# Two transposes of combine weights one period later, and one copy two places later, in a gated attention plus soft-MoE kernel

## The chip, the cores and the metric

The kernel runs on one core of one Trainium2 chip. The metric is device time in microseconds (us) of one execution. Everything is float32.

## The reference

The kernel computes a gated linear attention and, on its output, a soft mixture of experts:

```python
# attention: 4 batches, 8 heads, 768 steps, head size 48
f = 1.0 / (1.0 + np.exp(-f_logit))
for t in range(S):
    state = f[:, :, t, :, None] * state + np.einsum('bhd,bhe->bhde', k[:, :, t], v[:, :, t])
    y[:, :, t] = np.einsum('bhd,bhde->bhe', q[:, :, t], state)
# soft MoE on x = y as 3072 tokens x 384; 8 experts, 4 slots each, hidden size 1024
logits = x @ phi                                   # 3072 x 32
d = softmax over tokens (logits); slot_input = d.T @ x
slot_out[e] = np.maximum(slot_input[e] @ w1[e], 0.0) @ w2[e]
c = softmax over slots (logits);  out = c @ slot_out
```

(The two softmaxes are written out in the reference with the maximum subtracted and 1e-9 added to the sum.)

## The kernel before

**Pairs and periods.** The 32 pairs of batch and head are worked on two at a time, as 16 head pairs, four for each of the 4 batches. One head pair's work on TensorE is one period. In the order of TensorE's queue a period holds: the logits `pl` of an earlier pair (L461), the transpose `kt` of the decayed keys (L369), the transpose `xt` of an earlier pair's output (L440), the scores `sc` in two halves of 12 matmul instructions (L381), the key-value products `kv` (L415), and the outputs `y`, first within chunks (L406) and then across chunks (L429). Around it ScalarE (ACT) makes the gates (`fb`, L332 and L336; `gb`, L343; `pb`, L346) and copies `yT` and `xb` out of PSUM; VectorE (DVE) makes the running sums `Lb` (L340), copies `kta` out of PSUM, masks the scores (`scb`, L386) and scans the state (`sb`, L419); GpSimd (POOL) multiplies the decays into `kb` and `qb` (L349), and copies `pbx` and `pends`. A period's `kb` and `qb` are made one period before TensorE reads them.

**Once for each batch** three chains are added. The last `pl` of a batch is copied to `lt`; from it come the maximum, the exponential `et`, its transpose `te` (L479 to L481) and, two periods on, the slots' inputs `pi` (L504, 24 matmul instructions a batch). From the same `lt` comes the combine softmax: transpose `tl` (L479 to L481), maximum, subtraction and exponential into `ce` (L531, L534, L537), sum and reciprocal in `cm` (L541 to L544), the multiplication of `ce` by `cm` on GpSimd (L547, called `cdiv` in the plan), the transpose of `ce` on TensorE, `ct` (L553, two instructions), and the copy of `ct` into `cT` on ScalarE. `cT` is read only by the final combination, `pf` (L717), near the end.

**The order of the work** on each engine is made by a planner (`Plan.run`). Each operation has the engines that may do it with a duration, what it reads and writes, and a `due` time; operations given while `plan.fixed` is true run on their engine in the order of `due`. So `due` is not a time at which something happens on the chip; it is the sort key of the queue. One period counts `T = 7.0` in these numbers. `soft(b, (z0, z1))` (L832) writes down the combine chain of batch b: everything up to `cdiv` is due from z0 on, and `ct` and `cT` are due at z1 and z1 + 0.6. `mixture` (L849) calls it for batches 0 to 2; the last batch's chain is given elsewhere. The chain of the last batch's logits, from `gmax` to `psi`, is given in L930 to L948, and ends in `si`, the input of the experts' first layer `up` (L627). PSUM is handed out as 3 large and 2 small tiles (L233), kinds a and b; `kt`, `sc`, `y`, `xt`, `ct` and `te` of the last batch take large ones, `pl`, `kv`, `tl`, `pi`, `psi` small ones.

**Loads** are issued on SyncE's queue (SP) in one order: the inputs f, k, q and v of each pair, and between them the expert weights w1 and later w2. Each weight load is also tied to an operation (L1022 to L1029): it waits for the one which, in the plan, ended last before the load was to begin. A change of the plan so changes which operation a weight load waits for, and can change the order of loads.

**The end**: `up` (L627), `turn` (L644), the second layer `po` (L672), the combination `pf` (L717), and stores.

Of the kernel before, what the change touches and what calls it, by code (L numbers as in the profile page):

```python
# [74 lines left out]
class Plan:  # L75
# [22 lines left out]
    def op(self, name, engs, fn, *args, r=(), w=(), x=(), due=0.0, take=(), free=(), kb=0, home=False, ni=0):  # L98

        name, mode = name if isinstance(name, tuple) else (name, None)  # L100
        deps = set()
        for key in r:
            if key in self.writer:
                deps.add(self.writer[key])
        for key in (*w, *x):
            if key in self.writer:
                deps.add(self.writer[key])
            deps.update(self.readers.get(key, ()))
        fixed = self.fixed and "SP" not in engs
        o = Op(len(self.ops), name, engs, fn, args, due, deps, take, free, kb, home, ni, mode, fixed)  # L110
        self.ops.append(o)
        for key in w:
            self.writer[key] = o
            self.readers[key] = []
        for key in r:
            self.readers.setdefault(key, []).append(o)
        for key in (*r, *w):
            self.uses.setdefault(key, []).append(o)
        return o
# [90 lines left out]
T = 7.0  # L210
# [5 lines left out]
def gla_soft_moe_kernel(ctx: ExitStack, tc: tile.TileContext, q, k, f, v, vt, phi, w1, w2, out):  # L216
# [11 lines left out]
    def P(shape, name, dt=F32):  # L228
        return pool.tile(shape, dt, tag=name, name=name)
# [34 lines left out]
    lt = P([128, 192], "lt")  # L264
# [271 lines left out]
    def c_exp(o):  # L536
        nc.scalar.activation(ce, ce, AF.Exp)  # L537
# [190 lines left out]
    op = plan.op  # L728
# [4 lines left out]
    def warm(due, n, us=0.9):  # L733
# [11 lines left out]
        L=(-99, -98), dk=(-97, -95), dq=(-96, -94.5), mask=(-94.3, -92),  # L745
# [86 lines left out]
    def soft(b, z, after=()):  # L832

        CT, tl = ("ct", b), ("tl", b)
        op(("tl", "square"), {"PE": 0.35}, l_tr, lt, tl, r=["lt", *after], w=[tl], due=z[0], take=[(tl, "b")], ni=6)
        op("cmax", {"DVE": 0.36}, c_max, tl, r=[tl], w=["cm"], due=z[0] + 1.2)
        op("csub", {"DVE": 0.36}, c_sub, tl, r=[tl, "cm"], w=["ce"], due=z[0] + 1.3, free=[tl])
        op("cexp", {"ACT": 0.37}, lambda o: c_exp(o), r=["ce"], w=["ce"], due=z[0] + 2.2)
        op("csum", {"DVE": 0.7}, c_sum, r=["ce"], w=["cm"], due=z[0] + 5.2)
        op("cdiv", {"POOL": 0.55}, c_div, r=["ce", "cm"], w=["ce"], due=z[0] + 5.9)  # L840
        plan.fixed, was = plan.fixed or b == L, plan.fixed
        op(("ct", "square"), {"PE": 0.25}, c_tr, b, CT, r=["ce"], w=[CT], due=z[1], take=[(CT, "a")], ni=4)
        plan.fixed = was
        op("cte", {"ACT": 0.54}, c_copy, b, CT, r=[CT], w=[("cT", b)], due=z[1] + 0.6, free=[CT])

    L = B - 1
    XB = {b: [("xb", b % 2, p) for p in range(PPB)] for b in range(B)}

    def mixture(b, z):  # L849

        key = ("pl", b)
        op("lte", {"ACT": 0.34}, l_copy, key, r=[key], w=["lt", ("plfree", b + 1)], due=z + 4.1, free=[key])
        mx, sm = (nmx[:, 0:1], sms[:, 0:1]) if b == 0 else (nmb[:, 0:1], sms[:, 1:2])
        MX, SM = ("nmx0", "sms0") if b == 0 else ("nmb0", "sms1")
        op("gmax", {"DVE": 0.3}, g_max, lt, mx, r=["lt"], w=[MX], due=z + 5.5)
        op("gexp", {"ACT": 0.52}, g_exp, lt, mx, sm, r=["lt", MX], w=["et", SM], due=z + 5.9)
        key = ("te", b)
        op(("te", "square"), {"PE": 0.35}, l_tr, et, key, r=["et"], x=[("el", b % 2)], w=[key], due=z + T + 4, take=[(key, "b")], ni=6)
        op("ele", {"ACT": 0.34}, el_copy, b, key, r=[key], w=[("el", b % 2)], due=z + T + 5, free=[key])
        if b:  # L860
            op("j1", {"DVE": 0.1}, join_1, r=["nmx0", "nmb0"], w=["nmb1"], due=z + T + 3.8)
            op("j2", {"ACT": 0.5}, join_2, r=["nmx0", "nmb0", "nmb1"], w=["nmb2"], due=z + T + 4.1)
            op("j3", {"DVE": 0.5}, join_3, r=["nmb1", "nmb2", "sms1"], w=["nmx0", "sms0"], due=z + T + 5.5)
            op("j4", {"POOL": 0.6}, join_4, r=["nmb2"], w=["pin0"], due=z + 3 * T + 1.5)
        key = ("pi", b)
        op(("pi", "strips"), {"PE": 1.5}, slots_in, b, key, r=[*XB[b], ("el", b % 2)], w=[key], due=z + 3 * T + (3.5 if b < L - 1 else 5.2), take=[(key, "b")], ni=48)
        if b:
            op("j5", {"DVE": 0.65}, join_5, key, r=[key, "nmb2"], w=["pin0"], due=z + 3 * T + (5.5 if b < L - 1 else 6), free=[key])
        else:
            op("pie", {"ACT": 0.55}, pin_copy, 0, key, r=[key], w=["pin0"], due=z + 3 * T + 4.3, free=[key])  # L870
        soft(b, (z + 2 * T + 3.8, z + 3 * T + (3.8 if b < L - 1 else 5.85)))

    op("lphi", {"SP": 0.45}, load, phs, phi, w=["phs"], due=5, kb=112)
    first_op, past_op, batch_from = [], [], []
    for b in range(B):
        for i in range(PPB * b, PPB * b + PPB):
            first_op.append(len(plan.ops))
            attention(i)
            past_op.append(len(plan.ops))
        batch_from.append(len(plan.ops))  # L880
        if b < L:
            mixture(b, (PPB * b + PPB) * T)
# [38 lines left out]
    z = NP * T + 4  # L921
    LG = ("pl", L)
# [5 lines left out]
    y = (NP - 1) * T  # L928
# [7 lines left out]
    op(("pi", "strips"), {"PE": 1.5}, slots_in, L, PI, r=[*XB[L], ("el", L % 2)], w=[PI], due=y + 5.6, take=[(PI, "b")], ni=48)  # L936
    for x, cs in enumerate((slice(0, 256), slice(256, DM))):
        op("pie", [{"ACT": 0.42}, {"DVE": 0.25}][x], pin_copy, 1, PI, cs, r=[PI], w=[("pin1", x)], due=y + 6.3, free=[PI])
    op("lte", {"DVE": 0.33}, l_copy, LG, r=[LG], w=["lt"], due=y + 5.53, free=[LG])
    op("tm", {"DVE": 0.1}, t_max, r=["nmx0", "nmx1"], w=["zr0"], due=y + 5.52)  # L940
    op(("tmt", "square"), {"PE": 0.15}, t_max_tr, r=["zr0"], w=["pg"], due=y + 4.8, take=[(("pg",), "a")], ni=2)
    op("tm2", {"DVE": 0.35}, t_max_2, r=["pg"], w=["gr"], due=y + 5.54, free=[("pg",)])
# [34 lines left out]
    for part in range(len(PARTS)):  # L977
# [9 lines left out]
        for shared in range(2):  # L987
# [7 lines left out]
            for key, eng in zip(keys, ("ACT", "DVE")):  # L995
                x0, n = (2 + key[2], 1) if shared else (2 * key[2], 2)
                step = 1 if part == 2 else n
                for x in range(x0, x0 + n, step):
                    op(
                        "oute", {eng: {"ACT": 0.14, "DVE": 0.07}[eng] + {"ACT": 0.45, "DVE": 0.61}[eng] * step}, out_copy, part, x, step,  # L1000
                        r=[key, ("upw", 1, 0), ("upw", 1, 1)], w=[("st", part, y) for y in range(x, x + step)], due=d + 0.05 + 0.001 * x, free=[key],
# [158 lines left out]
```

## Time and profile before

| | |
|---|---|
| time, median of 3 runs | 166.93 us (166.82 to 167.4) |
| the profiled execution | 167.51 us |
| its span, first to last instruction | 165.8 us |
| mean granted TensorE clock | 0.994 of full speed |
| busy, share of the span: PE, DVE, ACT, POOL | 93%, 70%, 57%, 54% |
| DMA, mean over the span | 326 GB/s; 390 to 400 GB/s from about 20 to 80 us |

How to read the rows: in the timeline a row gives the start in us from the span's start, the duration in us, the engine, the line, the operation with the tile it writes and those it reads, and in brackets the idle time of that engine just before it and what ended it. PE is TensorE's matmuls, PEld its weight loads, SPq the issuing of DMAs. In the table of waits a row gives who waited for whom: the total in us, how many times, and the longest. In the table by stretches each engine has its busy time in the stretch and the number of instructions in brackets. Matmuls are pipelined and their ends are modelled, so one matmul's row can overlap the start of the next; starts are the safer numbers.

### The profile page before, as it was taken

Reading aid. Unit: us, or ns where it says so; the run is one execution under the profiler, and the core shown is the slowest. Engines: PE = TensorE matmul, PEld = TensorE weight load, DVE = VectorE, ACT = ScalarE, POOL = GpSimd, SP = SyncE. Lnnn points to the kernel's source line nnn. Section 1 sums busy time; section 2 is a strip of 40 time slices with the busy share of each in tenths; the row PEclk is TensorE's granted clock in tenths of the full one; section 3 lists DMA queues with packets and bytes.
Section 4 is the critical chain, followed back from the end, with each engine's and each line's share of the span. In section 5 each row is a group of like instructions: output and inputs, shape, how many; then the busy total and the mean of one; then the engine's idle time right before and its main releaser. Section 6 shows DMA issues by size and latency. Waiting matters only on the chain.

```text
span 165.8 us, 6378 instructions
## 1 busy us (share of the span) xinstructions
PE 153.4 (93%) x2724; PEld 123.3 (74%) x2724; DVE 116.4 (70%) x165; ACT 94.0 (57%) x164; POOL 90.0 (54%) x87
## 2 busy tenths in 40 slices
PE   5899999999999999999998999999899999999830
PEld 2267878988988978898995988989655448788720
DVE  4799999989989895898997889839433216134240
ACT  4889688767877948687692963712512212124140
POOL 5117869889889885897989689680100000100000
PEclk9999999999999999999999999999999999999997
DMA  5999999999999999999998459999999794036784
GB/s 135 311 406 372 387 400 398 401 388 399 394 392 400 396 396 397 398 402 390 402 368 290 131 183 280 337 372 408 395 399 391 215 374 171 4 140 243 273 338 167
DMA packets 20609, 54.05 MB, mean 326 GB/s; under 512 B 2288, under 2 KB 2912, under 8 KB 20576
## 3 DMA queue, kind: packets, MB, share of 16 engines
q1 hardware_dynamic: 20432, 53.34, 86.6%
q8 instruction: 22, 0.36, 0.9%
q10 hardware_dynamic: 144, 0.26, 0.4%
q14 instruction: 11, 0.09, 0.2%
HBM read 48.87 MB, written 4.72 MB: 323 GB/s over the span
## 4 chain that ended last, share of the span: by engine, by line
PE 67%; DVE 14%; issue 5%; POOL 4%; DMA 3%; ACT 2%; SPq 1%; POOLq 0%; ACTq 0%; DVEq 0%
PE sc L381 10%; PE y L406 9%; PE po L672 7%; PE up L627 7%; PE y L429 6%; PE kv L415 5%; PE kt L369 5%; DVE Lb L340 5%; PE xt L440 4%; PE pl L461 3%; PE pf L717 3%; DMA qb<-in_q_dram 3%; DVE scb L386 3%; POOL ce L547 2%; PE pi L504 2%
## 5 line engine op out<-in xcount | busy, mean ns | idle before, releaser
L349 POOL TENSOR_TENSOR kb<-kb,gb 112x768 f32<-112x768 f32 x15 | 27.5, 1830 | 16.4 <-ACT gb L343 12.9
L340 DVE TENSOR_TENSOR_SCAN Lb<-starts,fb 112x768 f32<-112x768 f32 (+1 forms) x17 | 35.0, 2059 | 1.7 <-ACT fb L336 1.7
L386 DVE TENSOR_TENSOR scb<-sc,mask 128x768 f32<-128x768 f32 x32 | 29.2, 950 | 4.0 <-PE sc L381 4.0
L323 POOL COPY pbx<-pb 112x240 f32<-112x240 f32 x16 | 26.8, 1673 | 4.7 <-ACT pb L346 4.7
L381 PE MATMUL sc<-qb,kb 48*128 48x128 f32 x384 | 26.5, 282 | 1.1 <-DVE qb L349 0.5
L406 PE MATMUL y<-scb,va 128*48 128x128 f32 (+1 forms) x384 | 25.9, 276 | 0.0
L381 PEld LDWEIGHTS sc<-qb,kb 48*128 48x128 f32 x384 | 22.9, 187 | 3.9 <-DVE qb L349 1.0
L323 ACT COPY yT<-y 112x768 f32<-112x768 f32 x16 | 12.8, 798 | 20.6 <-PE y L429 20.6
L349 POOL TENSOR_TENSOR qb<-qb,pb 112x768 f32<-112x768 f32 x13 | 23.8, 1827 | 0.0
L406 PEld LDWEIGHTS y<-scb,va 128*48 128x48 f32 (+1 forms) x384 | 21.9, 130 | 0.9 <-DVE scb L386 0.6
L547 POOL TENSOR_TENSOR ce<-ce,cm 128x256 f32<-128x256 f32 x4 | 4.6, 1155 | 29.8 <-DVE cm L544 29.3
L323 DVE COPY kta<-kt 128x672 f32<-128x672 f32 x14 | 11.8, 846 | 7.6 <-PE kt L369 7.6
L343 ACT ACTIVATE gb<-Lb 112x768 f32<-112x768 f32 (+1 forms) x17 | 13.7, 805 | 4.9 <-DVE Lb L340 4.9
L336 ACT ACTIVATE fb<-fb,one 112x768 f32<-112x768 f32 (+1 forms) x17 | 15.2, 897 | 0.5
L332 ACT ACTIVATE fb<-fb 112x768 f32<-112x768 f32 (+1 forms) x17 | 13.7, 806 | 2.1 <-DMA fb<-in_f_dram 2.1
L429 PE MATMUL y<-qb,sb 48*48 48x128 f32 x320 | 14.6, 285 | 0.0
L415 PE MATMUL kv<-va,kta 128*64 128x48 f32 (+1 forms) x384 | 14.4, 220 | 0.0
L415 PEld LDWEIGHTS kv<-va,kta 128*64 128x64 f32 (+1 forms) x384 | 12.4, 130 | 2.6 <-ACT kta L323 0.8
L346 ACT ACTIVATE pb<-Lb 112x768 f32<-112x768 f32 (+1 forms) x17 | 13.5, 792 | 0.0
L429 PEld LDWEIGHTS y<-qb,sb 48*48 48x48 f32 x320 | 11.1, 162 | 2.7 <-DVE sb L419 2.4
L369 PE MATMUL kt<-ident,kb 112*128 112x112 f32 x96 | 12.7, 266 | 0.3 <-POOL kb L349 0.2
L419 DVE TENSOR_TENSOR_SCAN sb<-kv,pbx 112x288 f32<-112x288 f32 x16 | 12.0, 747 | 0.0
(154 smaller groups left out, 270.2 us busy)
## 6 DMA issues: line engine op xcount, KB each, us to landing
w1a<-in_w_dram SPq DMA_DIRECT2D x34, 384.0 KB, 7.4
kb<-in_k_dram SPq DMA_DIRECT2D x16, 384.0 KB, 7.2
fb<-in_f_dram SPq DMA_DIRECT2D x15, 384.0 KB, 7.1
qb<-in_q_dram SPq DMA_DIRECT2D x15, 384.0 KB, 7.3
va<-in_v_dram SPq DMA_DIRECT2D x16, 288.0 KB, 7.2
out_dram<-w1a SPq DMA_DIRECT2D x6, 512.0 KB, 3.6
scb<-in_w_dram SPq DMA_DIRECT2D x4, 384.0 KB, 6.6
out_dram<-w1a SPq DMA_DIRECT2D x5, 256.0 KB, 2.6
```

The source lines that it names most:

```text
L323: {"ACT": nc.scalar.copy, "DVE": nc.vector.tensor_copy, "POOL": nc.gpsimd.tensor_copy}[o.eng](dst, src)
L332: nc.scalar.activation(t, t, AF.Exp, scale=-1.0, accum_out=esum[:, n : n + 1])
L336: nc.scalar.activation(t, t, AF.Ln, bias=one[:PW])
L340: nc.vector.tensor_tensor_scan(Lb[i % N_L][:PW, cs], flat(starts)[:PW, cs], fb[i % N_F][:PW, cs], 0.0, op0=ALU.mult, op1=ALU.add)
L343: nc.scalar.activation(gb[i % N_G][:PW, cs], Lb[i % N_L][:PW, cs], AF.Exp)
L349: (nc.vector if o.eng == "DVE" else nc.gpsimd).tensor_tensor(t, t, by, op=ALU.mult)
L369: nc.tensor.transpose(u[:, C * m : C * m + PW], kb[i % N_K][:PW, C * m : C * m + C], ident[:PW, :PW])
L381: nc.tensor.matmul(u[:, 512 * r + C * m : 512 * r + C * m + C], kb[i % N_K][rs, cs], qb[i % N_Q][rs, cs], start=True, stop=True,)
L386: nc.vector.tensor_tensor(scb[i % N_SC][:, :, h], un["sc", i, h].rearrange("p (r x) -> p r x", r=2)[:, :, : 3 * C].rearrange("p r (m t) -> ...
L406: nc.tensor.matmul(u[rows(at), y_cols(m)], va[:, v0 : v0 + (D if at else 64)], scb[i % N_SC][:, r, h, m % 3], start=m % 3 == 0, stop=False ...
L415: nc.tensor.matmul(u[rows(r), :, m], ktb[i % N_KT][:, m, rows(r)], vb[i % N_V][:, m, r], start=True, stop=True)
L429: nc.tensor.matmul(u[at : at + D, y_cols(m)], sb[i % N_S][rs, :, m - 1], qb[i % N_Q][rs, C * m : C * m + C], start=False, stop=m in (2, 5) ...
```

## The change

Two due times change. In `mixture`, `ct` and `cT` of the batches 0 and 1 (b < L - 1, where L is 3) become due 7.0, one period, later; those of batch 2 stay. In the chain of the last logits, the copy `lte` of `pl` to `lt` on VectorE becomes due at y + 5.905 in place of y + 5.53, which puts it behind `ele` (due y + 5.9), the copy of the transposes `te` of the last exponential. No operation is added, removed or given to another engine.

```diff
@@ -868,7 +868,7 @@ (mixture)
-        soft(b, (z + 2 * T + 3.8, z + 3 * T + (3.8 if b < L - 1 else 5.85)))
+        soft(b, (z + 2 * T + 3.8, z + (4 * T + 3.8 if b < L - 1 else 3 * T + 5.85)))
@@ -936,7 +936,7 @@
-    op("lte", {"DVE": 0.33}, l_copy, LG, r=[LG], w=["lt"], due=y + 5.53, free=[LG])
+    op("lte", {"DVE": 0.33}, l_copy, LG, r=[LG], w=["lt"], due=y + 5.905, free=[LG])
```

**TensorE, batch 0, the period in which `pi` of batch 0 runs and the next one** (`kb_80` is pair 8's key tile, `kb_78` pair 9's). Before:

```order
L504 MATMUL pi<-xb_95,el_101 32x4x48 x2
L553 MATMUL ct<-ident,ce 128x128 x2
L369 MATMUL kt<-ident,kb_80 128x112 x6
L440 MATMUL xt<-ident,yT_92 128x112 x6
L381 MATMUL sc<-qb_83,kb_80 128x128 x12
```

After the change `kt` follows `pi` directly, and one period on:

```order
L461 MATMUL pl<-yT_93,phs 32x64 x2
L553 MATMUL ct<-ident,ce 128x128 x2
L369 MATMUL kt<-ident,kb_78 128x112 x6
L440 MATMUL xt<-ident,yT_93 128x112 x6
L381 MATMUL sc<-qb_81,kb_78 128x128 x12
```

`ct` has moved from between `pi` and `kt` to between `pl` and `kt` of the next pair. The same holds for batch 1, four periods later.

**ScalarE at the same place, batch 0.** Before, `cT` stood between the copy `pin` of the slots' inputs and `gb`; now it stands one period on, behind `lt`:

```order
 L323 COPY yT_93<-y 112x768
 L323 COPY pin<-pi 128x384
-L323 COPY cT<-ct 128x256
-L343 ACTIVATE gb_75<-Lb_71 112x768
-L346 ACTIVATE pb_77<-Lb_71 112x768
+L323 COPY lt<-pl 128x192
+L323 COPY cT<-ct 128x256
 L343 ACTIVATE gb_74<-Lb_70 112x768
```

The removed `gb_75` and `pb_77` rows stand again, unchanged in their order, between `pin` and the next `yT`.

**VectorE in the chain of the last logits.** Before:

```order
L471 TENSOR_REDUCE nmx<-pl 128x1
L579 TENSOR_REDUCE zr<-nmx 128x1
L323 COPY lt<-pl 128x192
L585 TENSOR_REDUCE gr<-pg 1x32
L586 COPY gr<-gr 1x96
L323 COPY el_102<-te 128x256
L592 COPY zr<-pg_1769 128x1
```

After:

```order
L471 TENSOR_REDUCE nmx<-pl 128x1
L579 TENSOR_REDUCE zr<-nmx 128x1
L585 TENSOR_REDUCE gr<-pg 1x32
L586 COPY gr<-gr 1x96
L323 COPY el_102<-te 128x256
L323 COPY lt<-pl 128x192
L592 COPY zr<-pg_1767 128x1
```

The copy `lt` is now behind the three small reductions and copies and behind `el_102`. On SyncE's queue one load of w1 and the load of `kb_80` in the middle of the loop change places, and so do two weight loads (`Lb_70`, `kb_79`) later; GpSimd's order is the same.

## The prediction

> **What bounds the kernel now.** I read the chain of waits first, then the busy time by stretches with the edges put at the two `pi` blocks, then the table of waits. The first row is the chain's share by engine, the next three are stretches of the span, the last is from the table of waits.
>
> ```profile
> PE 67%; DVE 14%; issue 5%; POOL 4%; DMA 3%; ACT 2%; SPq 1%; POOLq 0%; ACTq 0%; DVEq 0%
> 60.75:65.69 4.94, 4.74 (x73) 3.63 (x67) 2.83 (x3) 3.70 (x7) 3.22 (x2) 1.00 1.03 396
> 65.69:88.61 22.92, 22.92 (x436) 20.49 (x439) 21.07 (x29) 17.36 (x32) 20.62 (x17) 1.00 1.01 385
> 88.61:93.88 5.27, 4.67 (x71) 3.56 (x63) 3.69 (x5) 3.14 (x6) 3.55 (x3) 1.00 0.73 231
> PE ct L553 <- POOL ce L547: 0.8, 2, 0.6
> ```
>
> PE is the first column after the length. Between the two blocks it is busy all the time (22.92 of 22.92 us); it idles 0.20 us beside the first `pi` and 0.60 beside the second. The wait row names the first two: both times `ct` waits for `cdiv`. So from 60 us to the last logits the kernel is as long as TensorE's queue, and what TensorE does not wait there the end should have, if nothing else is late next. Behind the logits TensorE goes on with `up` and `po`, so a shift reaches the end.
>
> **Part 1: `ct` leaves its old place.** Timeline rows of both blocks:
>
> ```profile
> 61.51 0.47 PEld L504 LDWEIGHTS pi<-xb,el 64*32 64x32 f32 x12 [0.31 <-issue]
> 62.56 0.44 PE L553 MATMUL ct<-ident,ce 128*128 128x128 f32 x2 [0.20 <-POOL ce L547]
> 62.84 0.74 PE L369 MATMUL kt<-ident,kb 112*128 112x112 f32 x6
> 63.41 0.74 PE L440 MATMUL xt<-ident,yT 112*128 112x112 f32 x6
> ...
> 89.37 0.47 PEld L504 LDWEIGHTS pi<-xb,el 64*32 64x32 f32 x12 [0.31 <-issue]
> 90.83 0.44 PE L553 MATMUL ct<-ident,ce 128*128 128x128 f32 x2 [0.60 <-POOL ce L547]
> 91.68 0.74 PE L440 MATMUL xt<-ident,yT 112*128 112x112 f32 x6
> ...
> 69.09 0.79 PE L369 MATMUL kt<-ident,kb 112*128 112x112 f32 x6
> 69.72 0.74 PE L440 MATMUL xt<-ident,yT 112*128 112x112 f32 x6
> ```
>
> Without `ct`, `kt` comes behind `pi`. The last weights of `pi` are loaded at 61.51 + 0.47 = 61.98. Inside `pi` a change of the tile's rows cost 0.31 of issue; I take the same for the change to `kt`: 62.29. A `kt` with no transpose ahead takes 0.63 until `xt` starts (69.09 to 69.72), so `xt` starts at 62.92 in place of 63.41: 0.49 earlier. The second block: 89.37 + 0.47 + 0.31 + 0.63 = 90.78 in place of 91.68: 0.90 earlier. Nothing else holds `kt`: its `kb` was made a period before.
>
> **Part 2: `ct` in its new place**, between `pl` and `kt`. Batch 0's `ce` is then over 6 us old, so it waits for nothing. The nearest row is `tl`, three transposes of the same width at the same place two periods earlier:
>
> ```profile
> 54.16 0.33 PE L479 MATMUL tl<-ident,lt 128*128 128x128 f32 x1
> 54.33 0.27 PE L480 MATMUL tl<-ident,lt 128*128 128x128 f32 x1
> 54.44 0.27 PE L481 MATMUL tl<-ident,lt 128*64 128x128 f32 x1
> ...
> 69.64 0.86 ACT L343 ACTIVATE gb<-Lb 112x768 f32<-112x768 f32 x1
> 69.92 0.86 DVE L323 COPY kta<-kt 128x672 f32<-128x672 f32 x1 [0.46 <-PE kt L369]
> 70.38 1.61 PE L381 MATMUL sc<-qb,kb 48*128 48x128 f32 x24
> 70.58 1.82 POOL L349 TENSOR_TENSOR kb<-kb,gb 112x768 f32<-112x768 f32 x1 [0.59 <-ACT gb L343]
> 75.39 0.79 PE L369 MATMUL kt<-ident,kb 112*128 112x112 f32 x6
> ...
> 63.04 0.37 ACT L323 COPY cT<-ct 128x256 f32<-128x256 f32 x1
> 63.30 0.85 ACT L343 ACTIVATE gb<-Lb 112x768 f32<-112x768 f32 x1
> ```
>
> Starts step 0.17 and 0.11, so `ct`'s two put `kt` 0.28 later; `kt` then takes 0.57 (62.84 to 63.41) and not 0.63: 0.22 us a batch on TensorE's path, 0.44 for both. On ACT `cT` now stands between `lt` and `gb`, with `gb`, `pb` and all of the period queued behind it; it costs 0.26 there (63.04 to 63.30), so `gb` is 0.26 later against a TensorE that is 0.22 later. What waits for `gb` is POOL's `kb`, done at 70.58 + 1.82 = 72.40 and wanted by the `kt` at 75.39: 3 us of cover, and the price is nothing. `ct` also holds a large PSUM tile until `cT` is copied, about 69.64 + 0.37 = 70.01, as it starts where `gb` did; the first to want a tile behind `kt` and `xt` is `sc`, at 70.38 + 0.22 = 70.60. Cover 0.6 us; nothing. At the old place `cT` no longer holds `gb` back, which only gives POOL time.
>
> Net of parts 1 and 2: 0.49 + 0.90 - 0.44 = 0.95 us. From below: the modelled idle alone, 0.20 + 0.60 = 0.80. From above: if the change from `pi` to `kt` has no issue gap of 0.31, 0.62 more, 1.57. I take 0.95, since the gap stands in every `pi` block.
>
> **Part 3: `lt` behind `el`.** Rows of the last logits:
>
> ```profile
> 118.35 0.36 DVE L471 TENSOR_REDUCE nmx<-pl 128x1 f32<-128x192 f32 x1 [1.90 <-PE pl L461]
> 118.82 0.35 DVE L323 COPY lt<-pl 128x192 f32<-128x192 f32 x1
> 119.28 0.42 ACT L474 ACTIVATE et<-pl,nmx 128x192 f32<-128x192 f32 x1 [0.81 <-DVE lt L323]
> 119.67 0.24 DVE L586 COPY gr<-gr 1x96 f32<-1x96 f32 x1
> 119.84 0.33 PE L479 MATMUL te<-ident,et 128*128 128x128 f32 x1 [0.53 <-ACT et L474]
> 120.32 0.38 PE L589 MATMUL pg<-one,gr 1*128 1x1 f32 x2
> 120.63 3.19 PE L504 MATMUL pi<-xb,el 128*32 128x192 f32 x48
> ```
>
> `et` reads `pl` and `nmx` and still started only 0.11 after `lt` ended (119.17 to 119.28); ACT stood idle 0.81 for it, and TensorE 0.53 for `et`. With `lt` moved, it can start 0.11 after `nmx`: 118.71 + 0.11 = 118.82, 0.46 earlier, and `te` at 119.38. The next in TensorE's queue is `pg`, from `gr`, which VectorE ends at 119.67 + 0.24 = 119.91 in both kernels, as it waits for a transpose and not for `lt`. With the same lag of 0.11 `pg` starts at 120.02 in place of 120.32, and the long `pi` behind it 0.30 earlier. So 0.30 of the 0.46 is kept; `gr` is late next. From below 0.10, if `pg` needs 0.20 of issue as it did behind `te` (119.84 + 0.17 + 0.11 = 120.12, to 120.32); from above 0.46. VectorE does `lt` behind `el` now and ahead of `zr`, the copy of `pg` that ends in the weights `wd` of `psi`; `psi` stands behind the whole of `pi`, 3.19 us, so 0.35 of `lt` is covered.
>
> **The sum**: 0.95 + 0.30 = 1.25 us, bounds 0.90 and 2.03. The profiled execution took 167.51 with a span of 165.8; its span should become about 164.55 and it 166.26. The median of the runs is 0.58 lower than this execution, so the forecast goes from the median: 166.93 - 1.25 = 165.68.
>
> **The rivals.** *First, the gap is closed but VectorE takes it back.* VectorE and POOL are busy 21.07 and 20.62 of 22.92 us, so neither has much left. Three rows that bear on them:
>
> ```profile
> 60.35 1.75 DVE L340 TENSOR_TENSOR_SCAN Lb<-starts,fb 112x768 f32<-112x768 f32 x1
> 60.58 1.93 POOL L547 TENSOR_TENSOR ce<-ce,cm 128x256 f32<-128x256 f32 x1 [0.48 <-PE y L429]
> 80.41 2.38 DVE L340 TENSOR_TENSOR_SCAN Lb<-starts,fb 112x768 f32<-112x768 f32 x1
> 116.60 0.62 POOL L547 TENSOR_TENSOR ce<-ce,cm 128x256 f32<-128x256 f32 x1 [5.24 <-DVE cm L544]
> ```
>
> `cdiv` takes 0.62 alone and 1.93 beside a scan (it ends at 62.51, 0.41 behind the scan's 62.10), and a scan takes 1.75 or 2.38. POOL moves against VectorE with the change (`gb` is freed of `cT`, then held by it). If every scan behind the moves came out at 2.38, 0.63 longer, 0.46 would vanish in the idle time ahead of `kta` and 0.17 would reach TensorE; in the six other periods of batches 2 and 3 that is 1.02 of the 1.25: 166.7. Against it: by the sums above, POOL moves only 0.04 against TensorE at the new place. The Trainium skill, page "SBUF — State Buffer", section "SBUF: two separate sides", says that VectorE and GpSimd share a pair of ports as an exclusive lock, held for the whole instruction by whoever starts first. The stretched `cdiv` agrees with it; by it this rival needs POOL's multiplication to reach further into the scan than now, and it would also be the reason that `ct` had to wait at all.
>
> *Second, only one place pays.* If a load or an ACT gate ties the loop after the first move, its 0.49 - 0.22 is lost, and with `pg` at its low bound the rest is 0.90 - 0.22 + 0.10 = 0.78: 166.15, just within half a percent. For it speaks a load:
>
> ```profile
> 77.75 0.33 SPq L327 DMA_DIRECT2D fb<-in_f_dram  x1
> 85.32 0.85 ACT L332 ACTIVATE fb<-fb 112x768 f32<-112x768 f32 x1
> 88.37 0.80 ACT L323 COPY yT<-y 112x768 f32<-112x768 f32 x1 [1.15 <-PE y L429]
> fb<-in_f_dram SPq DMA_DIRECT2D x15, 384.0 KB, 7.1
> ```
>
> Issued at 77.75 and landing 7.1 later (84.85), it is there only 0.47 before use, with DMA at 385 GB/s. Against it: ACT idles 1.15 before the next work that TensorE is behind.
>
> *Third, slower: the input loads come late.* SP's order changes at a weight load beside `kb_80`, and weight loads wait for other operations than before; SP is in order, so each f, q and k behind a weight load waits too. The `fb` above has 0.47 + 1.15 = 1.62 us; it decides from there on, and outweighs the gain from 2.87 us. A hold of 4 us would give 166.93 - 1.25 + (4 - 1.62) = 168.06. Against it: the number of loads ahead of `fb` is the same, and the stream has been full, so a hold must first drain it.
>
> **How the numbers follow.** Forecast (gain 0.90 to 2.03): 0.68. First rival 0.13, second 0.13, third 0.06. Half a percent, about what a measurement can tell from no change, is 0.83 us: the forecast is faster throughout, the second rival lies at the edge and counts a third as faster, the first is within it. Faster 0.72, same 0.22, slower 0.06. The likeliest's own range is 164.9 to 166.0; the top has little for it. To hold 8 in 10 with the rivals: 165.0 to 166.7.
>
> **What would show it.** Right: no `ct` row with idle before it in batches 0 and 1; the stretches from `pi` to the next `kv` 0.49 and 0.90 shorter, the periods with the moved `ct` 0.22 longer; `et` released by `nmx` at 0.11, with `pi` of the last batch released by `gr`. Wrong: a PE row behind the move that waits for DVE `kta`, for ACT or for a DMA, or scans of 2.3 us in the periods behind it; in the end, a `pi` that starts no earlier against `pl` than before, 2.28 us after `nmx` started.

## The result, and the profile after

The changed kernel takes 165.82 us (median of 13 runs, 165.5 to 166.63) and the kernel before, beside it on the same chip, 167.3 us (13 runs, 166.8 to 167.74). The ratio is 0.9925 with a 95% interval of 0.9911 to 0.994: 1.25 us faster, within 1.00 and 1.49. (The two medians are 1.48 apart; the ratio, taken over all runs, gives the 1.25.) The profiled execution took 165.64 us, with a span of 163.9 us. The kernel before is at 167.3 here and not at the 166.93 of the three runs shown first, so 167.3 is what the comparison goes by.

The chain of waits of the changed kernel, its share by engine:

```profile
PE 79%; DVE 7%; DMA 3%; issue 3%; ACT 2%; SPq 1%; DVEq 0%; ACTq 0%
```

GpSimd (4% before) has left the chain and VectorE's share has halved (14% before). The three stretches answering to those shown of before, each from the start of a `pi` block to the next `kv`, and what lies between; the columns are start, end and length, and then the busy time of PE, PEld, DVE, ACT and POOL:

```profile
60.04:64.42 4.38, 4.38 (x69) 3.34 (x61) 2.76 (x3) 3.25 (x6) 3.15 (x2) 1.00 1.04 396
64.42:87.64 23.22, 23.22 (x439) 20.78 (x440) 21.18 (x29) 17.72 (x33) 20.66 (x17) 1.00 1.03 392
87.64:92.02 4.38, 4.38 (x69) 3.34 (x61) 3.74 (x5) 3.04 (x5) 3.77 (x3) 1.00 0.87 263
```

TensorE is now busy for the whole of all three. The two `pi` stretches have become equal, 4.38 us in place of 4.94 and 5.27, and the one between, which holds the moved `ct`, is 0.30 longer. The first edge of before was placed too late: its `kv` starts at 65.62 and not at 65.69. By starts the first stretch of before is 4.87 and the middle one 22.99, so the stretches became 0.49 and 0.89 shorter and the middle one 0.23 longer. Timeline rows of both old places and of the first new one:

```profile
60.80 0.47 PEld L504 LDWEIGHTS pi<-xb,el 64*32 64x32 f32 x12 [0.31 <-issue]
61.58 0.58 PEld L369 LDWEIGHTS kt<-ident,kb 112*128 112x128 f32 x6 [0.31 <-issue]
62.22 0.74 PE L440 MATMUL xt<-ident,yT 112*128 112x112 f32 x6
67.89 0.44 PE L553 MATMUL ct<-ident,ce 128*128 128x128 f32 x2
68.16 0.74 PE L369 MATMUL kt<-ident,kb 112*128 112x112 f32 x6
68.44 0.39 ACT L323 COPY cT<-ct 128x256 f32<-128x256 f32 x1
68.71 0.87 ACT L343 ACTIVATE gb<-Lb 112x768 f32<-112x768 f32 x1
69.66 1.82 POOL L349 TENSOR_TENSOR kb<-kb,gb 112x768 f32<-112x768 f32 x1 [0.85 <-ACT gb L343]
...
88.40 0.47 PEld L504 LDWEIGHTS pi<-xb,el 64*32 64x32 f32 x12 [0.31 <-issue]
89.18 0.58 PEld L369 LDWEIGHTS kt<-ident,kb 112*128 112x128 f32 x6 [0.31 <-issue]
89.81 0.74 PE L440 MATMUL xt<-ident,yT 112*128 112x112 f32 x6
95.49 0.44 PE L553 MATMUL ct<-ident,ce 128*128 128x128 f32 x2
```

Neither `ct` row has idle time in front of it. Behind the second old place the change has one idle row that before has not, two periods on. By the plan, `kv` takes a small PSUM tile there, and `te` of the next batch holds one until ScalarE has copied it to `el`:

```profile
105.23 0.72 PEld L415 LDWEIGHTS kv<-va,kta 128*64 128x64 f32 x23 [0.17 <-ACT el L323]
```

From the `sc` before it to this `kv` it is 1.60 us there (from 103.64), and 1.55 in before. The last logits:

```profile
116.76 0.36 DVE L471 TENSOR_REDUCE nmx<-pl 128x1 f32<-128x192 f32 x1 [1.91 <-PE pl L461]
117.21 0.42 ACT L474 ACTIVATE et<-pl,nmx 128x192 f32<-128x192 f32 x1 [0.34 <-DVE nmx L471]
118.08 0.24 DVE L586 COPY gr<-gr 1x96 f32<-1x96 f32 x1
118.36 0.42 DVE L323 COPY el<-te 128x256 f32<-128x256 f32 x1
118.43 0.29 PEld L589 LDWEIGHTS pg<-one,gr 1*128 1x128 f32 x2 [0.38 <-PE te L481]
118.70 0.35 DVE L323 COPY lt<-pl 128x192 f32<-128x192 f32 x1
118.74 3.19 PE L504 MATMUL pi<-xb,el 128*32 128x192 f32 x48
```

`et` is now released by `nmx`, and `pg` starts 0.11 behind the end of `gr` (118.32).

To put all runs side by side, the table cuts each trace at the same five events. Starts are subtracted from starts: the first `pi` block (pi0), the second (pi1), `nmx` of the last logits, and `up`; "xt" is the time from a `pi` block to the `xt` behind it.

| kernel | start to pi0 | pi0 to xt, pi1 to xt | pi0 to pi1 | pi1 to nmx | nmx to up | up to end | ratio to before, 95% interval |
|---|---|---|---|---|---|---|---|
| before | 60.75 | 2.66, 3.07 | 27.86 | 29.74 | 6.93 | 40.52 | 1 |
| the change | 60.04 | 2.18, 2.17 | 27.60 | 29.12 | 6.63 | 40.51 | 0.9925 (0.9911 to 0.994) |
| e1: only the ct moves | 60.06 | 2.18, 2.17 | 27.60 | 29.11 | 6.92 | 40.51 | 0.9944 (0.9926 to 0.9962) |
| e2: only lt moves | 60.20 | 2.66, 3.05 | 27.86 | 29.72 | 6.63 | 40.49 | 0.9988 (0.9964 to 1.0011) |
| e3: only ct of batch 0 | 59.98 | 2.18, 3.27 | 27.60 | 29.95 | 6.92 | 40.55 | 1.0005 (0.9984 to 1.0026) |
| e4: only ct of batch 1 | 60.56 | 2.67, 2.18 | 27.86 | 29.12 | 6.93 | 40.53 | 0.9973 (0.9948 to 0.9998) |
| e5: old places, nothing to wait for | 60.21 | 2.39, 2.39 | 27.59 | 29.07 | 6.92 | 40.51 | 0.9942 (0.9926 to 0.9959) |
| e6: lt only behind gr | 60.75 | 2.18, 2.18 | 27.60 | 29.11 | 6.63 | 40.51 | 0.9916 (0.9898 to 0.9934) |
| e7: gr's copy twice | 60.10 | 2.18, 2.18 | 27.60 | 29.13 | 6.91 | 40.56 | 0.9964 (0.9948 to 0.9979) |
| e8: ct behind psi | 60.73 | 2.18, 2.18 | 27.37 | 28.84 | 6.91 | 40.95 | 0.9921 (0.9907 to 0.9935) |
| e9: ct in two gaps, pg's tile | 60.73 | 2.17, 2.17 | 27.37 | 28.86 | 6.87 | 41.37 | 0.9944 (0.9921 to 0.9968) |
| e10: e3 and half a load | 60.43 | 2.17, 3.10 | 27.59 | 29.78 | 6.92 | 40.58 | 0.9989 (0.9968 to 1.001) |
| e11: before and half a load | 60.62 | 2.67, 3.04 | 27.86 | 29.72 | 6.93 | 40.47 | 1.0002 (0.9978 to 1.0025) |
| e12: ct in two gaps, te's tile | 60.26 | 2.17, 2.18 | 27.36 | 28.86 | 6.68 | 41.44 | 0.9914 (0.9889 to 0.9939) |

From before to the change the span fell by 1.9 us, but 0.71 of that lies ahead of pi0, before anything that the change moves; this start lies between 59.98 and 60.75 in the fourteen traces, and not by kernel (e6, which begins as the change does, has 60.75). The part from pi0 to the end is what the change can be held to: 0.26 + 0.62 + 0.30 + 0.01 = 1.19 us.

### The profile page after: what moved, and what is told of

Read it like the earlier page. It is cut to its first block, busy times and chain, and to the rows that moved or that the text cites. A ratio compares the mean times of both kernels' runs of the same rounds, so it can differ in the third digit from the quotient of the medians.

```text
span 163.9 us, 6383 instructions
## 1 busy us (share of the span) xinstructions
PE 153.2 (93%) x2724; PEld 123.3 (75%) x2724; DVE 115.9 (71%) x165; ACT 93.9 (57%) x164; POOL 90.0 (55%) x87
## 4 chain that ended last, share of the span: by engine, by line
PE 79%; DVE 7%; DMA 3%; issue 3%; ACT 2%; SPq 1%; DVEq 0%; ACTq 0%
PE sc L381 13%; PE y L406 12%; PE y L429 7%; PE po L672 7%; PE up L627 7%; PE kv L415 7%; PE kt L369 5%; PE xt L440 5%; PE pl L461 4%; PE pi L504 4%; PE pf L717 3%; DVE Lb L340 3%; DMA qb<-in_q_dram 3%; PE turn L644 1%; DVE scb L386 1%
## 5 line engine op out<-in xcount | busy, mean ns | idle before, releaser
L369 PEld LDWEIGHTS kt<-ident,kb 112*128 112x128 f32 x96 | 9.6, 140 | 3.2 <-DVE kb L349 1.4
```

The costliest lines, as they stand in the source:

```text
L369: nc.tensor.transpose(u[:, C * m : C * m + PW], kb[i % N_K][:PW, C * m : C * m + C], ident[:PW, :PW])
```

## The experiments

### Each part alone: e1 and e2

The theory: two independent gains, 0.95 from the transposes and 0.30 from the last logits. e1 has the first line of the diff alone, e2 the second.

> Only the transposes ct of batches 0 and 1 move one period later; the copy lt stays ahead of the last exponential. Theory (TensorE's waits and the two transitions are all of it): 0.49 + 0.90 - 0.44 = 0.95 us less than before, ratio 0.9943; in the trace xt behind pi starts 2.17 us behind the last weights of pi's first half or earlier, that is pi to xt 2.18 us in batch 0 and 1 (before: 2.66 and 3.07). Rival (the change in the order of loads or a better start does it): the gaps between pi and xt shrink as said but the whole differs from 0.95 by more than 0.4, or the time is won ahead of 60 us. Rival (VectorE takes it back): less than 0.5 us.

> Only the copy lt moves behind el; ct stays. Theory: et is released by nmx, the long pi of the last batch starts 0.30 us earlier against nmx (1.98 in place of 2.28), and the whole is 0.30 us shorter, ratio 0.998. Rival (the long pi is not on the path, or the copies behind it are late next): the pi starts earlier but si does not, and the time is that of before within 0.1 us.

e1 measured 0.9944, and its trace has the changed loop with the old tail (6.92 from `nmx` to `up`). e2 has the old loop with the new tail (6.63); its ratio, 0.9988, has an interval that holds 1, so the time alone would not show the 0.30, and the trace does. The pieces of both add up to the change's.

### Is it the wait, or the place? e5

The transposes of batches 0 and 1 stay at their old place, and read a constant in place of `ce`:

```diff
-            nc.tensor.transpose(u[:, 128 * x : 128 * x + 128], flat(ce)[:, 128 * x : 128 * x + 128], ident)
+            nc.tensor.transpose(u[:, 128 * x : 128 * x + 128], flat(emask if b < L - 1 else ce)[:, 128 * x : 128 * x + 128], ident)
```

> The kernel before, with ct of batches 0 and 1 at their old place, but transposing a constant tile that is there from the start instead of the combine weights (so those two batches' outputs are wrong; work and order on every queue are the same, loads too). Theory: without the wait ct follows pi at 0.31, then kt 0.28 and xt 0.57 behind: pi to xt 2.39 in place of 2.66, and 2.39 in place of 3.07: 0.27 + 0.68 = 0.95 us less than before, as much as moving them. Rival (the place matters, a transpose between pi and kt costs more than one between pl and kt, or the order of loads made the gain): less than 0.7.

Timeline rows of e5, first place:

```profile
60.21 1.61 PE L504 MATMUL pi<-xb,el 128*32 128x192 f32 x24
61.75 0.44 PE L553 MATMUL ct<-ident,emask 128*128 128x128 f32 x2
62.60 0.74 PE L440 MATMUL xt<-ident,yT 112*128 112x112 f32 x6
```

`ct` itself stands 0.31 behind the end of `pi`'s weights (60.21 + 1.23 to 61.75) and costs the same 0.22 as at the new place: 2.39 from `pi` to `xt` against 2.17. The ratio is that of e1. All order and all loads are those of before, so what the move of `ct` is worth is the wait for GpSimd's product, and neither the place nor the order of loads.

### One transpose at a time: e3 and e4

```diff
-        soft(b, (z + 2 * T + 3.8, z + 3 * T + (3.8 if b < L - 1 else 5.85)))
+        soft(b, (z + 2 * T + 3.8, z + (4 * T + 3.8 if b == 0 else 3 * T + (3.8 if b < L - 1 else 5.85))))
```

That is e3; e4 has `b == 1`.

> Only ct of batch 0 moves, batch 1's stays and lt stays. Theory: 0.49 - 0.22 = 0.27 us less than before, and the wait of batch 1's ct is still 0.6 us, since POOL's multiplication there hangs on VectorE and so on TensorE, which are all earlier by the same. Rival (the second wait is set by something that does not move with TensorE, a load or POOL's own queue): the gain comes back as a longer wait at batch 1's ct, 0.87 in place of 0.60, and the time is that of before.

> Only ct of batch 1 moves. Theory: 0.90 - 0.22 = 0.68 us less than before, ratio 0.9959; with e3 it adds up to e1. Rival (only one place pays): e1 is no better than this one, 0.95 in both or 0.68 in both.

e4 did what was expected (0.62 from pi1 to nmx). The trace of e3 gained 0.26 up to pi1 and lost 0.21 directly behind it: the `ct` of batch 1, left at its old place, waited 0.80 in place of 0.60. So in these traces the two moves give 0.05 and 0.62 apart (from pi0 to nmx) and 0.88 together. Timeline rows of e3 ahead of that `ct`:

```profile
82.81 1.82 POOL L349 TENSOR_TENSOR kb<-kb,gb 112x768 f32<-112x768 f32 x1 [0.50 <-ACT gb L343]
84.76 1.83 POOL L349 TENSOR_TENSOR qb<-qb,pb 112x768 f32<-112x768 f32 x1
85.61 0.84 ACT L332 ACTIVATE fb<-fb 112x768 f32<-112x768 f32 x1 [1.30 <-DMA fb<-in_f_dram]
86.52 0.63 POOL L323 COPY pbx<-pb 112x240 f32<-112x240 f32 x1
86.54 0.65 DVE L542 TENSOR_SCALAR cm<-cm 128x8 f32<-128x8 f32 x1
87.58 1.62 PE L504 MATMUL pi<-xb,el 128*32 128x192 f32 x24
87.79 1.75 DVE L340 TENSOR_TENSOR_SCAN Lb<-starts,fb 112x768 f32<-112x768 f32 x1
88.46 1.48 POOL L547 TENSOR_TENSOR ce<-ce,cm 128x256 f32<-128x256 f32 x1
90.00 0.44 PE L553 MATMUL ct<-ident,ce 128*128 128x128 f32 x2 [0.80 <-POOL ce L547]
```

`fb` waits 1.30 us for its load, and `qb` starts 0.13 after `kb` has ended (84.63). With all of TensorE 0.26 earlier, the scan starts 0.21 behind pi1 (0.01 before) and the product 0.88 behind it (0.71 before). The next theory: the loads come when the full DMA stream brings them, and do not move with TensorE.

### The loads: e10, and its control e11

e3 with half of one load left out, that of pair 12's queries, so that it and all behind it come earlier by half a load; e11 has the same edit in the kernel before.

```diff
-            op("lq", {"SP": 0.45}, load, qb[i % N_Q], q[i], w=Q, due=z - 12, kb=384)
+            op("lq", {"SP": 0.45}, load_half if i == 12 else load, qb[i % N_Q], q[i], *([HALVES[0]] if i == 12 else []), w=Q, due=z - 12, kb=384)
```

> Batch 0's ct alone moved (as in e3_ct_b0), and of one query load, that of pair 12, only the first half of the columns is loaded (the result of that pair is left wrong): 192 KB less in the full stream, so this load and those behind it land about 0.49 us earlier; nothing else changes on any queue. My theory: in e3_ct_b0 the wait of batch 1's ct grew from 0.60 to 0.80 because the loads of q and f land at times that do not move with TensorE. Then qb starts straight behind kb on GpSimd, fb starts 0.3 to 0.5 earlier, the wait of batch 1's ct falls back to 0.60 or less, the gain of 0.26 comes through, and the ratio is 0.998. Rival: the wait hangs on VectorE and GpSimd blocking one another beside pbx, whatever the loads do: the wait stays at 0.80 and the ratio at 1.0005.

> The kernel before with the same halved load of pair 12's queries (its result is left wrong), as the control: there qb started straight behind kb and fb without idle time ahead of it, so by my theory loads set nothing, batch 1's ct waits 0.60 as before and the ratio is 1.000. If the halved load by itself speeds the stretch up, the ratio falls to 0.998 here too, and e10_b0_half says nothing on the moved ct.

The same rows of e10:

```profile
84.66 0.83 ACT L332 ACTIVATE fb<-fb 112x768 f32<-112x768 f32 x1
85.05 1.83 POOL L349 TENSOR_TENSOR qb<-qb,pb 112x768 f32<-112x768 f32 x1
88.06 1.75 DVE L340 TENSOR_TENSOR_SCAN Lb<-starts,fb 112x768 f32<-112x768 f32 x1
90.27 0.44 PE L553 MATMUL ct<-ident,ce 128*128 128x128 f32 x2 [0.63 <-POOL ce L547]
```

`qb` follows `kb` without a gap, `fb` waits for nothing, the scan stands 0.04 behind pi1 (88.02), and the wait is 0.63. From pi0 to nmx e10 takes 57.37 us; before takes 57.60, e3 57.55 and the control 57.58. So where the loads come in time, most of the gain of 0.26 comes through.

That the half load brought them in time is not shown. In e6 the first transpose is moved as in e3 and all loads are whole, and it has the same rows: `qb` without a gap, no wait of `fb`, the scan 0.04 behind pi1. With whole loads and the same first move, the wait for `fb` differs by itself from trace to trace: 0 in e6, 0.42 in e7, 0.59 in the change, 1.04 in e1, 1.30 in e3. And TensorE gets to pi0 at 59.98 in e3, the earliest of the fourteen, and 0.45 later in e10, about what the half load was to win (0.49).

Which load counted in e3 the rows do tell. In e1, with the same move of the first transpose, `fb` comes 1.04 late and nothing is lost:

```profile
85.41 0.84 ACT L332 ACTIVATE fb<-fb 112x768 f32<-112x768 f32 x1 [1.04 <-DMA fb<-in_f_dram]
86.62 0.46 DVE L542 TENSOR_SCALAR cm<-cm 128x8 f32<-128x8 f32 x1
87.68 1.75 DVE L340 TENSOR_TENSOR_SCAN Lb<-starts,fb 112x768 f32<-112x768 f32 x1
```

The scan stands 0.02 behind pi1 (87.66). In e3 VectorE has no idle time ahead of the scan, so the scan did not wait for `fb`; it stood behind the scaling of `cm` (L542), which took 0.65 in place of 0.46. That one ran beside GpSimd's `pbx`, which came later because `qb` did. The query load of e3 was issued at 76.67 and landed 7.9 later, at 84.6, just ahead of `qb` (84.76); in e1 it landed at 84.4, and `qb` (84.65) had no gap. In e12, further down, the query load also lands at 84.6, `qb` starts at 84.74, L542 takes 0.58 and the scan is 0.15 late. So the late load that costs something here is the query load, by way of `pbx` and VectorE.

Of the nine traces with the first transpose moved, `qb` had to wait for its load in two, e3 and e12. Whether the kernel of e3 loses its gain in most executions, or only its profiled one did, is therefore open: its ratio (1.0005) has an interval that ends at 0.9984, just where a gain of 0.27 would lie, and that of e10 (0.9989) holds 1 and overlaps it.

In the change the `fb` load is late too, and without effect:

```profile
84.97 0.84 ACT L332 ACTIVATE fb<-fb 112x768 f32<-112x768 f32 x1 [0.59 <-DMA fb<-in_f_dram]
87.41 0.80 ACT L323 COPY yT<-y 112x768 f32<-112x768 f32 x1 [0.53 <-PE y L429]
```

ScalarE waits 0.59 for the load and then 0.53 for TensorE, where it had idled 1.15: the delay went into idle time, and there is no `ct` behind pi1 any more that would wait for what follows from it.

### What sets the start of the last pi: e6 and e7

e6 puts `lt` behind `gr` but ahead of `el` (due y + 5.545). e7 does `gr`'s second copy twice:

```diff
         nc.vector.tensor_copy(gr[:, 1:4], gr[:, 0:1].broadcast_to([1, 3, NS]))
+        nc.vector.tensor_copy(gr[:, 1:4], gr[:, 0:1].broadcast_to([1, 3, NS]))
```

> The changed kernel, with the copy lt not behind el but right ahead of it, behind the copy gr. Theory: what counts is that the last exponential no longer stands behind lt, not that el does not; el is then some 0.35 us later, but it is wanted only by the second half of the long pi, 1.5 us on. Same as the changed kernel within 0.1 us. Rival (el is late next): 0.35 us slower than the changed kernel.

> The changed kernel with the small copy gr (0.24 us on VectorE, 0.28 from start to start) done twice. Theory (gr is what is late next in the chain of the last logits): the pg behind it, the long pi and the end are all 0.28 us later than in the changed kernel, so nearly all of the 0.30 is gone. Rival (pg waits for the transposes te, as its idle row says, and gr has room): less than 0.1 us.

Timeline rows of e6:

```profile
118.78 0.24 DVE L586 COPY gr<-gr 1x96 f32<-1x96 f32 x1
119.14 0.29 PEld L589 LDWEIGHTS pg<-one,gr 1*128 1x128 f32 x2 [0.38 <-PE te L481]
119.21 0.40 DVE L323 COPY el<-te 128x256 f32<-128x256 f32 x1
119.44 0.47 PEld L504 LDWEIGHTS pi<-xb,el 128*32 128x32 f32 x12
```

And of e7, whose line 590 is line 589 of the others:

```profile
118.78 0.29 PEld L590 LDWEIGHTS pg<-one,gr 1*128 1x128 f32 x2 [0.65 <-PE te L481]
118.81 0.35 PE L590 MATMUL pg<-one,gr 1*128 1x1 f32 x2 [0.41 <-DVE gr L587]
119.09 0.47 PEld L504 LDWEIGHTS pi<-xb,el 128*32 128x32 f32 x12
```

In e6 `el` starts 0.15 later against `nmx` than in the change (1.75 behind it, not 1.60; the expectation had 0.35), and the tail does not lengthen. In e7 `el` is as late (1.76), and one more copy of `gr` moves `pg` and `pi` by 0.28, the length of the copy with its start. So `gr` and not `el` sets the last `pi`, by way of `pg`, as the prediction said. The name in the idle row, `te`, is not the one that matters: in e7 the last weights of `te` were loaded 0.65 before, and the row of the matmul behind these weights names `gr`. (The expectation's reason, that only the second half of `pi` wants `el`, does not fit the kernel: in L504 the first weights of `pi` are already `el`.) `pi` follows `pg` by 0.30 or 0.31 in all of these.

### A still later place: e8, e9 and e12

The remaining price is TensorE's 0.22 a batch. In these three `ce` of each batch is kept in its own place in `cT`, so that the transposes may wait for the end. e8 puts them behind the last `psi`. e9 puts one pair of transposes behind the first `pg` and one behind `te`, where TensorE waits anyway, into the unused half of `pg`'s tile, with one copy on ScalarE behind the last `xb`. e12 does the same in `te`'s tile, with the first pair ahead of `te` (cut to the queue's lines; `...` marks what is left out):

```diff
+    op(("ct", "square"), {"PE": 0.25}, c_tr2, 0, TE, r=[("cT", 0)], w=[("ct", 0)], due=y + 4.9, take=[(TE, "a")], ni=4)
-    op(("te", "square"), {"PE": 0.35}, l_tr, et, TE, r=["et"], x=[("el", L % 2)], w=[TE], due=y + 5, take=[(TE, "a")], ni=6)
+    op(("te", "square"), {"PE": 0.35}, l_tr, et, TE, r=["et", ("ct", 0)], x=[("el", L % 2)], w=[TE], due=y + 5, ni=6)
+    op(("ct", "square"), {"PE": 0.25}, c_tr2, 1, TE, r=[("cT", 1), TE], w=[("ct", 1)], due=y + 5.05, ni=4)
...
+    op("cte", {"ACT": 0.65}, c_copy2, TE, r=[("ct", 0), ("ct", 1), ("el", L % 2)], w=[("cT", 0), ("cT", 1)], due=y + 6.02, free=[TE])
```

> The changed kernel with ct of batches 0 and 1 moved further, behind the last psi, where TensorE waits for si; the combine weights of each batch are kept in the batch's own cT tile, so that they are not overwritten. Theory: TensorE's 0.22 us a batch in the loop are gone, and of the 0.44 in the new place about 0.4 stands in TensorE's wait for si: 0.3 to 0.44 us less than the changed kernel. Rival (the copies or a PSUM tile there hold up the first up): no gain, or up to 0.3 us slower than the changed kernel.

> The change, with the transposes of batches 0 and 1 in TensorE's idle time of the last logits' chain: those of batch 0 behind pg, those of batch 1 behind te, both into the unused bank of pg's tile, one copy of 512 columns on ScalarE behind the last xb. The waits there are 0.27 and 0.38 us on the weight-load side (from the trace of the change) and two transposes take 0.22, so the chain from nmx to up stays 6.63 and the loop loses its two times 0.22: 0.44 us less than the change, that is 1.70 below before, a ratio of 0.990. If the holes do not hold them (a change of tile or of the PSUM bank costs issue time there, or pg is held up behind them), nmx to up grows by what does not fit, up to 0.44, and the ratio is the change's 0.9925. In the run with all four behind psi the last stores came 0.44 later; if that belongs to the moved cT and not to the shift of psi, it comes back here and the ratio is 0.993.

> As the run with the transposes in the holes, but both go into the unused bank of te's tile, so that gr, which reads pg's tile, is behind neither of them; el, which reads te's, is behind the second, and the run with lt ahead of el showed that el may be 0.35 us late for nothing. If the 0.24 lost from nmx to up in the holes' run came from gr waiting for the transposes in its tile (its row stood 0.21 later against nmx), nmx to up is 6.63 to 6.70 here, and start of the first pi to up is 0.40 to 0.45 shorter than in the change. If it came from TensorE's own time, it stays at 6.87. The last store on ScalarE's queue took 1.20 and 2.28 us in the two runs with these late transposes and 0.38 in all others, all with up 0.4 to 0.5 later against their start than the change; if that comes with the moved transposes it is over 1 us again and the time no better than the change's (ratio 0.9925 or above); if it was the shift of the end against the loads, it is 0.38 and the ratio is 0.990.

In all three the two stretches of the loop are 0.23 or 0.24 and 0.26 to 0.28 shorter than in the change, as it should be without the transposes. e8 pays 0.28 of that back behind `psi`. e9 pays 0.24 back in the tail, and its rows show by what:

```profile
118.17 0.28 DVE L593 TENSOR_REDUCE gr<-pg 1x32 f32<-1x128 f32 x1 [0.67 <-PE pg L558]
118.88 0.29 PEld L597 LDWEIGHTS pg<-one,gr 1*128 1x128 f32 x2 [0.17 <-DVE gr L594]
```

`gr` stands 1.21 behind `nmx` in place of 1.00 in the change, because it now waits for the transposes (L558) that were written to its tile behind the value it reads: this program's waits go by tile, not by column. e12, with `gr` free of them, takes 6.68 from `nmx` to `up`; from pi0 to `up` it is 0.45 shorter than the change. That part of e12's expectation held, and it is the third time that `gr` decides.

Yet none of the three is shown faster than the change by the time, and the column "up to end" says where it went: 0.44, 0.86 and 0.93 more. The last stores go out on two queues, SyncE's and ScalarE's. Rows of them in the change and then in e8; the three numbers behind each are the shortest, the middle and the longest time of one issue in ns:

```profile
L725 SPq DMA_DIRECT2D out_dram<-w1a x11: 332/382/1149, 145.0 to 158.3; - x11
L725 ACTq DMA_DIRECT2D out_dram<-w1a x1: 380/380/380, 157.5 to 157.5; - x1
...
L725 SPq DMA_DIRECT2D out_dram<-w1a x11: 332/383/531, 145.5 to 158.8; - x11
L725 ACTq DMA_DIRECT2D out_dram<-w1a x1: 1202/1202/1202, 158.0 to 158.0; - x1
```

Issuing ScalarE's store takes 1.20, 2.28 and 2.01 us in e8, e9 and e12, and 0.38 in the eleven others. In those eleven it is SyncE's last store that takes long, 1.13 to 1.16, against 0.53 to 0.57 in the three. So one of the last issues is long in every kernel, and the three with late transposes differ in the queue that has it and, in two of them, in its length. In e8 it is not ScalarE's store that ends last: it lands 4.2 after its start, at 162.1, and SyncE's last one at 163.4. e12 rules out that the longer end came from a later `up` (`up` is earlier there than in the change). Why all this comes with the late transposes is not known, and that the long issue is what lengthens the end is not shown; giving ScalarE's store to SyncE's queue was not tried. Against before, e12 is at 0.9914 and the change at 0.9925, with intervals that overlap: no version here is shown to beat the change.

## Why the prediction was right

**What bounds the kernel** held: what TensorE no longer waited came out at the end, 1.19 us of the trace and 1.25 of the time, for a sum of 1.25. The parts agree to a few hundredths; that the time gives 1.25 to the digit is luck, with an interval from 1.00 to 1.49.

**Part 1** gave 0.49 and 0.90 at the two old places; the traces have 2.66 to 2.18 and 3.07 to 2.17, that is 0.48 and 0.90. The step that carried it was the choice of 0.31 of issue between `pi` and `kt`, for which before had no row. It is there now, as the idle time of `kt`'s weight loads, 0.31 both times; without it the gain would have been the upper bound. (The first stretch, with its edge at 65.69, was read 0.07 too long, as said above; the sums go by the rows and do not use it.) The Trainium skill, page "TensorEngine Tiling (Array Packing)", section "Key Properties", says that a change of the tiling mode drains TensorE, and gives no figure; the trace agrees, with 0.31 at this place.

**Part 2**, 0.22 a batch, is what is left over: from pi0 to pi1 0.26 = 0.48 - 0.22. From pi1 to `nmx` it is 0.62 against 0.90 - 0.22 = 0.68. Of the 0.06 between them, 0.05 lie at the `kv` that waits for `el` (1.60 in place of 1.55 from `sc` to `kv`). This is small, and it is one of the signs that the prediction had named as wrong: a row of TensorE behind the move that waits for ScalarE. Its free items stayed free: `gb` follows `cT` by 0.27, and `kb` ends at 71.48 and holds nobody up.

**Part 3**, 0.30 of 0.46, with `gr` late next, came out at 0.30. The lower bound, 0.10, depended on whether `pg` starts 0.11 or 0.20 behind its releaser, and it was 0.11; the upper, 0.46, on `gr` not being late next, and it was.

**The first rival**, VectorE taking it back, did not occur: the six scans behind the first move, from 66 to 103 us, add up to 12.16 us in both kernels (the shortest 1.75, the longest 2.38 before and 2.43 now), and no row of TensorE in the loop waits for `kta`. The lock of ports that the Trainium skill describes (page "SBUF — State Buffer", section "SBUF: two separate sides") is, by these scans, no more costly after the move than before it. The rows do not show GpSimd's product fully shut out by the scan: before the change it ended 0.41 behind the scan, and alone it takes 0.62.

**The second rival**, a load or gate that lets only one place pay, named the right load, `fb`, and the right reserve, ScalarE's idle 1.15. The load did come late, by 0.59, and the reserve held. The first reserve was smaller than said: the prediction took the middle time to landing, 7.1, for this one load, which landed 7.5 after its issue, at 85.3, just as it was wanted (85.32). And the load that came nearest to costing something was the query load beside it: in the trace of e3, with only the first transpose moved, it took 0.21 of 0.26. The prediction added the two places as if each stood alone; that is right for the change, and in that one trace it is wrong for half of it.

**The third rival**, loads held by SyncE's new order, did not occur: with `fb` landing just in time the reserve was ScalarE's 1.15 and not 1.62, and 0.53 of it is left in the change.

**What was off** is the span of the profiled execution, 164.55 forecast and 163.9 measured. The forecast took the start from the one trace of before, whose 60.75 to pi0 is at the top of the fourteen; 0.71 us lie there. The median, from which the time was forecast, was itself 0.37 higher in the comparison.

## What to carry to other kernels

Where one engine has no idle time but a few tenths beside one instruction, ask what that instruction waits for and whether its result is wanted soon: moving it behind finished work gives the wait back and costs only its own time there. Whether the gains of such moves add up depends on what sits between them: here a load that came late in one trace took back 0.21 of 0.26, and in e1 another came 1.04 late and took nothing. One trace does not tell which of these a kernel does as a rule; compare traces that share the stretch. And the engine named as the releaser of an idle row can be the wrong one: lengthening the suspected step by one copy settled it in one run.

## What the runs showed of the hardware that was not expected

- Among the last stores of every kernel one issue takes over 1 us: SyncE's last one, 1.13 to 1.16, in eleven kernels, and ScalarE's, 1.20 to 2.28, in three that differ from the change in where four transposes and their copies stand, 35 to 40 us earlier. The other queue's issue is then 0.38 or 0.53 to 0.57. The cause is open.
- The end that a row shows is not always what a waiting engine goes by: in the rows of e6 the copy `el` ends at 119.61, and the weight load of `pi`, which reads `el`, starts at 119.44. Before the change the two stand 0.22 apart in the same sense (120.85 and 120.63). So a rival of the kind "`pi` waits for `el`" cannot be judged from these ends; e6 and e7, which have the same late `el` and differ by 0.28 in `pi`, judge it.
